# A fused attention and feed-forward kernel: a PSUM bank for the unread products, shared q/k copies, and later zeros

## The chip, the cores and the metric

One core of one Trainium2 chip. The metric is the device time in microseconds (us) of one execution; the median of several executions is compared. Profiles are of one further execution, and their times count from the first instruction of the program.

## What is computed

Chunked attention, and a gated feed-forward layer on its output. There are 4 batches, 8 heads, 768 positions of 64 elements, and 8 memory rows per head. A chunk of 32 queries sees the 8 memory rows and a window of keys from 16 before the chunk to 8 after it.

```
for c in range(nc):
    k_full = concat([mem_k, k[:, :, l_start:r_end]])
    v_full = concat([mem_v, v[:, :, l_start:r_end]])
    a = softmax(scale * q_c @ k_full.T)
    out[:, :, c_start:c_end] = a @ v_full
x = out.transpose(0, 2, 1, 3).reshape(3072, 512)
return (relu(x @ w_gate) * (x @ w_val)) @ w_out
```

The inputs are float32; w_gate and w_val are 512 x 1536, w_out is 1536 x 512. The sizes of chunk and windows are constants of the reference.

## The kernel before

**Tiles.** The 3,072 rows of x are 24 tiles of 128 rows (a = 0 to 23), six a batch. For each tile TensorE transposes q and k into PSUM (`qk_t`, L271; in the first batch two tiles at a time from one load, `pair_t`, L232), ScalarE or VectorE copies them to qT and kT (`qk_copy`, `pair_copy`), TensorE makes the scores (`scores`, L297, 32 small matmuls), VectorE takes the maximum (L322) and subtracts it (L329), ScalarE exponentiates (L337), VectorE sums (L341), inverts (L345) and normalises to p_n (L352). TensorE transposes p_n (L358), a copy makes pT, and TensorE multiplies with the values (`values`, L368) into xT_ps, which is copied to xT. The first batch's values are not loaded into their place by a DMA: they come as natural tiles v_n, are shifted by products with a banded identity (`shift`, L204) and copied into v_q, which lies in v_bd[0]; the memory values come in through vmem_0 (L374). For the later batches the values lie block-diagonal in v_bd[0] and v_bd[1], which must be zero beside the blocks: zeros (`zero`, L130), a load of 32 rows of each window by GpSimd's DMA queue (`load_v_rows`, L182), copies of 24 rows by VectorE (`upper`, L190), and the memory rows (`mem_rows`, L164; in batch 1 from SyncE's queue).

**Feed-forward.** Tiles go in eight blocks of 2 or 4. For a block and each of 12 slices of 128 of the 1,536 columns, TensorE makes g_ps and v_ps (`first`, L401, four matmuls each), ScalarE the relu (L413) and VectorE the product gvT (L419). Then each tile's output is 12 matmuls with w_out (L432), a copy by ScalarE and a store issued by ScalarE (L439).

**PSUM.** Eight banks: pool fps has 4 (g_ps, v_ps, out_ps, vs_ps), sps has 2 that hold one tile of scores, s_all (L138), and aps has 2 (all transposes and xT_ps).

**The order of the work** is made ahead by a planner in the kernel (`schedule`, L683): every piece is an `op` with its engines and planned costs in us, what it depends on, a priority tuple (smaller first), and what it takes from and gives back to `room`, the planned number of free buffers. The planner walks through planned time and gives each engine, whenever it is free, the first ready op. Its result is one fixed order of instructions for each engine; on the chip each engine works through its order and waits by semaphores. GpSimd issues the loads in the order of the list `loads` (L640 to L676), at most 8 in flight.

**Unread products.** While TensorE has nothing ready between planned times 1.3 and WARM = 22 (L678), the planner puts in matmuls of a zero tile `idle` (L468) whose result nobody reads (L141, L751). They write columns 256 to 383 of the second half of s_all; the scores use columns 0 to 255 of both halves.

**Zeros.** v_bd[1] is zeroed at the start in four pieces, one a head pair, by VectorE or ScalarE (`z1`, L470). Of v_bd[0], head pair 2 is zeroed at the start too (`z0`, L471); pairs 3, 0 and 1 hold the memory pattern and v_q until the first batch has used them, and are zeroed later in three pieces each (L472 to L475).

```
op("vm0", {"DVE": 0.5}, lambda e: nc.vector.tensor_copy(vmem_0, vmem_f), [("vml", 1.8)], prio=(-3,))
```

This copies the memory pattern, which SyncE's queue loads (`vml`), to vmem_0; `new_batch` (L259) copies the memory keys into kT before a batch's keys.

Of the kernel before, what the change touches and what calls it, by code (L numbers as in the profile page):

```python
# [19 lines left out]
def kernel(  # L20
# [12 lines left out]
    nc = tc.nc  # L33
# [50 lines left out]
    band = const.tile([128, BAND0 + 176], F16, name="band")  # L84
    ident_h = band[:, BAND0:BAND0 + 128]
    ident_b = const.tile([128, 128], BF16, name="ident_b")
    idle = const.tile([128, 128], BF16, name="idle")
    ident_f = const.tile([128, 128], F32, name="ident_f")
    w_gate_sb = const.tile([128, NFC, DFF], F16, name="w_gate_sb")
    w_val_sb = const.tile([128, NFC, DFF], F16, name="w_val_sb")  # L90
# [44 lines left out]
        else:  # L135
            eng.memset(x.rearrange("p c d -> p (c d)"), 0.0)

    s_all = sps.tile([128, 2, 512], F32, name="s_ps")  # L138

    def idle_product(N):  # L140
        nc.tensor.matmul(s_all[:, 1, 256:256 + N], lhsT=idle, rhs=idle[:, 0:N], start=True, stop=True)  # L141


    def mem_load():
# [151 lines left out]

    def scores(a):  # L297
        b, t = divmod(a, TPB)
        s = s_all
        keys = kT[b].rearrange("p h c s -> p h (c s)")  # L300
        for h2 in range(HP):
            m, par = h2 % 2, h2 // 2
            for g in range(4):
                c = 4 * t + g
                lo, hi = max(KW * c - 16, 0), min(KW * c + 48, NCH * KW)
                o0 = 64 * (2 * m + par) + lo - (KW * c - 16)
                for r in range(2):
                    d = slice(D * r, D * r + D)
                    nc.tensor.matmul(s[CH * g:CH * g + CH, r, o0:o0 + hi - lo],  # L309
                                     lhsT=qT[b][d, h2, CH * c:CH * c + CH],  # L310
                                     rhs=keys[d, h2, lo:hi], start=True, stop=True)
        S_ps[a] = s.rearrange("p a (h s) -> p a h s", s=64)[:, :, 0:HP, :]
# [154 lines left out]

    op("idle", {"DVE": 0.2}, lambda e: nc.vector.memset(idle, 0.0), prio=(-10,))  # L468
    for hp in range(HP):
        op(("z1", hp), {"DVE": 1.5, "ACT": 1.6}, lambda e, hp=hp: zero(engine[e], v_bd[1], hp), ["idle"], prio=(-1, hp), after=["warm2", "vmem_f"] + ["ib"] * (hp > 0))  # L470
    op(("z0", HP - 2), {"DVE": 1.5, "ACT": 1.6}, lambda e: zero(engine[e], v_bd[0], HP - 2), ["idle"], prio=(-1, HP), after=["ib", ("z1", 0)])  # L471
    for hp in (HP - 1, 0, 1):  # L472
        for c0 in range(0, NCH, 8):
            op(("z0", hp, c0), {"ACT": 0.6, "DVE": 0.55}, lambda e, hp=hp, c0=c0: zero(engine[e], v_bd[0], hp, c0, c0 + 8),
               ["vm0" if hp == HP - 1 else ("v", TPB - 1)], prio=(3, -hp) if hp == HP - 1 else (0.7, hp), after=[("v", 3)])  # L475
    op("warm", {"DVE": 0.15}, lambda e: nc.vector.memset(warm, 0.0), prio=(-9,))
    op("warm2", {"ACT": 1.5}, lambda e: nc.scalar.activation(warm, warm, ACT.Exp), ["warm"], prio=(-9,))
    op("vmem_f", {"DVE": 0.55}, lambda e: nc.vector.memset(vmem_f, 0.0), prio=(-8,), after=["warm"])
# [4 lines left out]
    op("kmt", {"PE": 0.25}, lambda e: mem_keys_t(), [("kml", 1.8), "if"], prio=(-5,), take=["aps"])  # L483
    op("kmc", {"ACT": 0.35}, lambda e: nc.scalar.copy(kmemT.rearrange("p b h m -> p (b h m)"), TMP.pop("kmem")),
       ["kmt"], prio=(-5,), give=["aps"])
    op("vm0", {"DVE": 0.5}, lambda e: nc.vector.tensor_copy(vmem_0, vmem_f), [("vml", 1.8)], prio=(-3,))
    for b in range(B):
        op(("new", b), {"DVE": 0.4}, lambda e, b=b: new_batch(b), ["kmc"], take=["kv"],
           prio=(-4.5,) if b == 0 else (1, TPB * b - 2, 0), after=[("t", TPB * b - 2, 0)] if b else [])
# [31 lines left out]
    for a in range(NT):  # L521
        b, t = divmod(a, TPB)
        last = t == TPB - 1
        for i in (1, 0):
            if b == 0:
                if t % 2 == 0:
                    for j in range(2):
                        op(("t", a + j, i), {"PE": 0.3}, lambda e, a=a, i=i, j=j: pair_t(a // 2, i, j),
                           [("pl", a // 2, i), "ib", ("new", b)], (1, a - i, -2 + j), ["aps"])
                        op(("tc", a + j, i), psum16(HP * 128), lambda e, a=a, i=i, j=j: pair_copy(a // 2, i, j, engine[e]),  # L530
                           [("t", a + j, i)], (1, a - i, -2 + j), (), ["aps"])
                continue
            if a >= LATE_QK:
                op(("t", a, i), {"SP": ISSUE}, lambda e, a=a, i=i: qk_transfer(a, i),
                   [(("qk", a, i), SLACK), ("new", b)],
                   (1, a - i, 0), ["kt"] if i else [], [("qk", LAND)], pace_t(a))
                if i:
                    op(("tc", a, i), {"DVE": (0.2, 0.29), "ACT": (0.52, 0.62)}, lambda e, a=a, i=i: qk_copy(a, i, engine[e]),
                       [(("t", a, i), LAND)], (1, a - i, 0), (), ["kt"])
                continue  # L540
            op(("t", a, i), {"PE": 0.24}, lambda e, a=a, i=i: qk_t(a, i), [("qk", a, i), "ib", ("new", b)],
               (1, a - i, 0), ["aps"], ["qk"], pace(max(a - i, 0)))
            op(("tc", a, i), psum16(HP * 128), lambda e, a=a, i=i: qk_copy(a, i, engine[e]), [("t", a, i)],
               (1, a - i, 0), (), ["aps"])
# [116 lines left out]
    for i in range(2):  # L661
        load(("wo", i), 768, 4.1, lambda i=i: load_out(i))
    for b in range(1, B):
        deps = ([("z0", HP - 2)] + [("z0", hp, c0) for hp in (HP - 1, 0, 1) for c0 in range(0, NCH, 8)] if b > 1 else [("z1", hp) for hp in range(HP)]) + ([("v", TPB * (b - NSET + 1) - 1)] if b > NSET else [])
        if b == 1:
            for n in range(2 * HP):
                op(("mr", b, n), {"SP": 0.72}, lambda e, n=n: mem_rows(nc.sync, 1, n),
                   deps + [(("vm", 0), 0.2), (("vm", 1), 0.2)], (0,))
        for par in range(2):
            load_v_op(b, par, deps)  # L670
        if b > 1:
            for n in range(2 * HP):
                load(("mr", b, n), 192, 0.22, lambda b=b, n=n: mem_rows(nc.gpsimd, b, n),
                     deps + [(("vm", 0), 0.2), (("vm", 1), 0.2)])
        for a, i in late[5 if b == 1 else 9 + 12 * (b - 1):21 + 12 * (b - 1)]:
            load_qk_op(a, i)  # L676

    WARM = 22.0  # L678

    def timed(d):  # L680
        return isinstance(d, tuple) and len(d) == 2 and isinstance(d[1], float)
# [1 line left out]
    def schedule():  # L683
        done, started, times = {}, set(), [0.7]
        free = {e: 0.7 for e in ("PE", "ACT", "DVE", "SP", "POOL")}
        queue_end, flying, gives = 0.0, [], []
        todo = {e: [] for e in free}
        order, n_load = [], 0
        names = lambda o: [d[0] if timed(d) else d for d in o["deps"]] + o["after"]
# [23 lines left out]
        while len(started) < len(ops) + len(loads):  # L713
# [8 lines left out]
            while moved:  # L722
                moved = False
                for e in ("POOL", "PE", "ACT", "DVE", "SP"):
                    if free[e] > t + 1e-9:
                        continue
                    if e == "POOL":
                        if n_load == len(loads):
                            continue
                        o = loads[n_load]  # L730
                        if len(flying) >= 8 or not ready(o, t):
                            continue
                        n_load += 1
                        key = o["key"]
                        if o["n"]:
                            end = t + 0.62 + 0.27e-3 * o["n"]
                            queue_end = max(queue_end, end + 0.8) + o["work"]
                            flying.append(queue_end + 1.0)
                            done[key] = queue_end + (1.2 if n_load < 8 else 2.4 if n_load < 45 else 6.0 if key[0] == "vl" else 4.0)
                        else:  # L740
                            end = done[key] = t + max(o["work"], 0.6)
                        fn = o["fn"]
                    else:
                        o = None
                        for _, key in todo[e]:
                            late_pe = e == "PE" and t > 36.0 and ops[key]["prio"][0] == 1
                            if ready(ops[key], t, MARGIN if late_pe else 0.0):
                                o = ops[key]
                                break
                        if o is None:  # L750
                            if e == "PE" and 1.3 < t < WARM:  # L751
                                order.append((t, lambda: idle_product(128)))
                                free[e] = t + (0.107 if t < 9.0 else 0.06)
                                heapq.heappush(times, free[e])
                            elif e == "PE" and t <= 1.3:
                                heapq.heappush(times, 1.31)
                            continue
# [62 lines left out]
```

## Time and profile before

| | |
|---|---|
| device time, three executions | 246.74, 247.69, 246.75 us; median 246.75 |
| the profiled execution | 248.35 us |
| its span, first to last instruction | 246.6 us |
| TensorE clock granted over the span | 1.0 |
| unread products (L141) in the trace | 152, busy 13.4 us |

In a profile, PE is TensorE's matmul, PEld its weight load, DVE VectorE, ACT ScalarE, POOL GpSimd and SP SyncE. A timeline row has the start, the duration, the engine, the line and operation, what is written and read, how many instructions were merged, and in brackets how long the engine had been idle before and what ended that; "issue" means that the profile shows nothing that it waited for. A row of waits has the sum, the number and the longest. The page shows the span in 40 slices of 6.17 us as digits, tenths of busy time. A windows row has the stretch, its length, and for PE, PEld, DVE, ACT and POOL the busy time and the number of instructions. A DMA queue row has packets, MB and the share of 16 engines.

### The profile page before, as it was taken

What the parts mean: (1) busy time and instruction counts of PE and PEld (TensorE: products, weight loads), DVE (VectorE), ACT (ScalarE), POOL (GpSimd) and SP (SyncE); (2) the same over time, 40 slices, a digit from 0 to 9 for tenths busy, and PEclk for the clock granted to TensorE, in tenths of its full rate; (3) what the DMA queues carried; (4) which work ended last, traced back from release to release, by engine and by line L of the source; (5) the groups of instructions that cost most, each with busy time, mean ns of one, the idle gap of its engine ahead of it and who ended that gap; (6) DMA issues with size and microseconds to landing.
All of it is one profiled execution on the core that took longest, in us unless ns stands there. A gap on an engine that the chain in (4) does not pass through costs nothing.

```text
span 246.6 us, 6706 instructions
## 1 busy us (share of the span) xinstructions
PE 237.7 (96%) x2789; PEld 145.2 (59%) x2789; DVE 154.4 (63%) x313; ACT 121.0 (49%) x269; POOL 77.5 (31%) x102
## 2 busy tenths in 40 slices
PE   7969799999999999999999999999999999999994
PEld 6858688887558744555544545554445444444873
DVE  5364687897989739999558999996342034320430
ACT  6564665967446435666325654463332232312432
POOL 8885779212985269319160000000000000000000
PEclk9999999999999999999999999999999999999999
DMA  6999999999999949999996421562001210002102
GB/s 70 173 178 202 201 160 155 191 133 113 147 187 181 102 98 129 131 130 165 103 190 91 45 45 23 130 130 45 3 0 41 90 43 0 0 27 103 43 3 85
DMA packets 96414, 25.19 MB, mean 102 GB/s; under 512 B 87424, under 2 KB 93312, under 8 KB 96384
## 3 DMA queue, kind: packets, MB, share of 16 engines
q0 software_dynamic: 76128, 14.65, 82.1%
q1 hardware_dynamic: 16656, 3.82, 15.1%
q10 hardware_dynamic: 3600, 6.29, 7.9%
q8 instruction: 22, 0.36, 0.6%
q14 instruction: 8, 0.07, 0.1%
HBM read 28.55 MB, written 6.29 MB: 141 GB/s over the span
## 4 chain that ended last, share of the span: by engine, by line
PE 93%; DVE 3%; DMA 1%; issue 1%; ACT 0%; SPq 0%; ACTq 0%
PE v_ps L407 26%; PE g_ps L407 26%; PE out_ps L432 24%; PE s_ps L141 4%; PE xT_ps L388 3%; PE s_ps L309 2%; PE qk_ps L275 2%; PE qk_ps L236 2%; PE pT_ps L358 2%; PE xT_ps L381 1%; PE vs_ps L215 1%; DMA kmem_f<-in_mem_k_dram 1%; PE xT_ps L374 1%; DVE mx L322 1%; DVE dif L329 1%
## 5 line engine op out<-in xcount | busy, mean ns | idle before, releaser
L419 DVE TENSOR_TENSOR gvT<-v_ps,g_relu 128x256 f16<-128x256 f32 (+1 forms) x96 | 52.9, 554 | 54.3 <-PE v_ps L407 40.8
L407 PE MATMUL v_ps<-xT,w_val_sb 128*128 128x256 f16 (+1 forms) x384 | 78.2, 326 | 0.0
L407 PE MATMUL g_ps<-xT,w_gate_sb 128*128 128x256 f16 (+1 forms) x384 | 78.1, 326 | 0.0
L413 ACT ACTIVATE g_relu<-g_ps 128x256 f16<-128x256 f32 (+1 forms) x96 | 47.2, 493 | 52.4 <-PE g_ps L407 51.1
L432 PE MATMUL out_ps<-w_out_sb,gvT 128*128 128x512 f16 (+2 forms) x300 | 65.8, 371 | 0.0
L407 PEld LDWEIGHTS <-w_gate_sb 128*128 128x128 f16 x384 | 36.4, 98 | 23.0
L407 PEld LDWEIGHTS <-w_val_sb 128*128 128x128 f16 x384 | 36.1, 98 | 22.4 <-issue 0.2
L432 PEld LDWEIGHTS <-gvT 128*128 128x128 f16 x300 | 27.8, 98 | 29.4
L79 ACT COPY o_sb<-out_ps 128x512 f32<-128x512 f32 (+2 forms) x25 | 14.2, 568 | 38.4 <-PE out_ps L432 28.3
L337 ACT ACTIVATE p_exp<-dif 128x256 f16<-128x256 f32 (+2 forms) x72 | 19.7, 343 | 10.4 <-DVE dif L329 9.9
L322 DVE TENSOR_REDUCE mx<-s_ps 128x8 f32<-128x512 f32 x24 | 16.5, 687 | 5.3 <-PE s_ps L309 4.8
L254 POOL DMA_DIRECT2D qk_b<-in_q_dram x18 | 16.3, 903 | 11.2 <-DMA v_bd<-in_v_dram 8.5
L81 DVE COPY v_bd<-v_bd 24x768 f16<-24x768 f16 (+1 forms) x48 | 18.0, 415 | 2.7 <-DMA v_bd<-in_v_dram 2.1
L254 POOL DMA_DIRECT2D qk_b<-in_k_dram x18 | 16.3, 908 | 5.2 <-DMA w_out_sb<-in_moe_w_out_dram 3.8
L341 DVE TENSOR_REDUCE sm<-p_exp 128x8 f32<-128x512 f16 x24 | 16.3, 677 | 2.3 <-ACT p_exp L337 2.1
L329 DVE TENSOR_TENSOR dif<-s_ps,mx 128x512 f32<-128x512 f32 x24 | 16.4, 682 | 0.9 <-PE s_ps L141 0.6
L352 DVE TENSOR_TENSOR p_n<-p_exp,rinv 128x512 f16<-128x512 f16 x24 | 16.5, 686 | 0.4
L141 PE MATMUL s_ps<-idle 128*128 128x128 bf16 x152 | 13.4, 254 | 3.0 <-DVE dif L329 1.6
L168 POOL DMA_DIRECT2D v_bd<-vmem x16 | 10.4, 658 | 15.6 <-DMA v_bd<-in_v_dram 15.1
L185 POOL DMA_DIRECT2D v_bd<-in_v_dram x12 | 11.0, 924 | 9.9 <-DVE dif L329 9.2
L141 PEld LDWEIGHTS <-idle 128*128 128x128 bf16 x152 | 11.6, 116 | 4.1 <-issue 2.4
L79 ACT CAST xT<-xT_ps 128x512 f16<-128x512 f32 x16 | 9.3, 583 | 6.9 <-PE xT_ps L388 3.8
(56 smaller groups left out, 172.3 us busy)
## 6 DMA issues: line engine op xcount, KB each, us to landing
out_dram<-o_sb ACTq DMA_DIRECT2D x23, 256.0 KB
qk_b<-in_k_dram POOLq DMA_DIRECT2D x18, 128.0 KB, 7.3
qk_b<-in_q_dram POOLq DMA_DIRECT2D x18, 128.0 KB, 7.0
v_bd<-in_v_dram POOLq DMA_DIRECT2D x6, 384.0 KB, 13.1
w_out_sb<-in_moe_w_out_dram POOLq DMA_DIRECT2D x2, 768.0 KB, 11.0
qk_p<-in_k_dram POOLq DMA_DIRECT2D x3, 256.0 KB, 5.8
qk_p<-in_q_dram POOLq DMA_DIRECT2D x3, 256.0 KB, 6.6
v_n<-in_v_dram POOLq DMA_DIRECT2D x6, 128.0 KB, 7.0
```

What stands on the lines that cost most here:

```text
L79: nc.scalar.copy(o, i)
L81: eng.tensor_copy(o, i)
L141: nc.tensor.matmul(s_all[:, 1, 256:256 + N], lhsT=idle, rhs=idle[:, 0:N], start=True, stop=True)
L254: nc.gpsimd.dma_start(qk_b[a, i], bass.AP(tensor=x.tensor, offset=x[b, 0, 128 * t, 0].offset, ap=[[D, 128], [S * D, H], [1, D]]))
L322: nc.vector.reduce_max(SM[a, "mx"], s4, axis=AX.X)
L329: nc.vector.tensor_tensor(out=SM[a, "dif"].rearrange("p (m r) a s -> p r m a s", r=2), in0=S_ps.pop(a).rearrange("p r (m a) s -> p r m a s ...
L337: nc.scalar.activation(p[:, :, :, s0:s0 + k1 - k0], dif[:, :, :, k0:k1], ACT.Exp, scale=SCALE)
L352: nc.vector.tensor_tensor(out=P_n[a], in0=SM.pop((a, "p")), in1=rinv_b, op=ALU.mult)
L407: nc.tensor.matmul(ps, lhsT=w[:, f, 128 * m:128 * m + 128], rhs=xTs[blk][:, f, :], start=(f == 0), stop=(f == NFC - 1))
L413: nc.scalar.activation(st["r", m], st.pop((0, m)), ACT.Relu)
L419: nc.vector.tensor_tensor(out=st["gv"][:, m, :], in0=st.pop((1, m)), in1=st.pop(("r", m)), op=ALU.mult)
L432: nc.tensor.matmul(st["o", t, c], lhsT=st["gv"][:, m, 128 * t:128 * t + 128], rhs=w_out_sb[:, m, c[0]:c[1]], start=(m == 0), stop=(m == ND ...
```

## The change

The unread products get a buffer of fps of their own, and 256 columns instead of 128; the planner counts one fps buffer less until just after WARM, which is 18 instead of 22. The scores take their tile from the pool for each tile instead of one fixed tile. For the first pair of tiles the copies of the first half go to ScalarE and those of the second half to VectorE. The early zeros of v_bd[1] are assigned to engines by head pair, and the zeros of head pair 2 of v_bd[0] move from the start to the later pieces. The copy to vmem_0 has another priority.

```diff
-    idle = const.tile([128, 128], BF16, name="idle")
+    idle = const.tile([128, 256], BF16, name="idle")
-    s_all = sps.tile([128, 2, 512], F32, name="s_ps")
-
     def idle_product(N):
-        nc.tensor.matmul(s_all[:, 1, 256:256 + N], lhsT=idle, rhs=idle[:, 0:N], start=True, stop=True)
+        if "idle" not in TMP:
+            TMP["idle"] = fps.tile([128, 512], F32, tag="fps", name="idle_ps")
+        nc.tensor.matmul(TMP["idle"][:, 0:N], lhsT=idle[:, 0:128], rhs=idle[:, 0:N], start=True, stop=True)
     def scores(a):
-        s = s_all
+        s = sps.tile([128, 2, 512], F32, name="s_ps")
     for hp in range(HP):
-        op(("z1", hp), {"DVE": 1.5, "ACT": 1.6}, ..., prio=(-1, hp), after=["warm2", "vmem_f"] + ["ib"] * (hp > 0))
-    op(("z0", HP - 2), {"DVE": 1.5, "ACT": 1.6}, lambda e: zero(engine[e], v_bd[0], HP - 2), ["idle"], ...)
-    for hp in (HP - 1, 0, 1):
+        op(("z1", hp), {"ACT": 1.5} if hp % 2 else {"DVE": 1.4}, ..., after=["warm2", "vmem_f"] + ["ib"] * (hp == 2))
+    for hp in (2, 3, 0, 1):
         for c0 in range(0, NCH, 8):
             op(("z0", hp, c0), {"ACT": 0.6, "DVE": 0.55}, ...,
-               ["vm0" if hp == HP - 1 else ("v", TPB - 1)], prio=(3, -hp) if hp == HP - 1 else (0.7, hp), after=[("v", 3)])
+               ["vm0" if hp > 1 else ("v", TPB - 1)], prio=(3, -hp) if hp > 1 else (0.7, hp), after=[("v", 3)])
-    op("vm0", {"DVE": 0.5}, ..., [("vml", 1.8)], prio=(-3,))
+    op("vm0", {"DVE": 0.5}, ..., [("vml", 1.8)], prio=(1, 0, 4.5))
-                        op(("tc", a + j, i), psum16(HP * 128), ...
+                        op(("tc", a + j, i), psum16(HP * 128) if t else {("ACT", "DVE")[j]: psum16(HP * 128)[("ACT", "DVE")[j]]}, ...
-    WARM = 22.0
+    WARM = 18.0
-        queue_end, flying, gives = 0.0, [], []
+        queue_end, flying, gives = 0.0, [], [(WARM + 0.15, "fps")]
+        room["fps"] -= 1
+        heapq.heappush(times, WARM + 0.15)
-                                order.append((t, lambda: idle_product(128)))
-                                free[e] = t + (0.107 if t < 9.0 else 0.06)
+                                order.append((t, lambda: idle_product(256)))
+                                free[e] = t + (0.213 if t < 9.0 else 0.11)
```

The loads of the later batches' values depend on the zeros as before, with the new pieces in the list. "..." within a line stands for text that is the same on both sides. Because the planner runs again, the orders change elsewhere too. The changed program has 69 unread products instead of 152; from the middle of the third batch's attention on, the orders on TensorE are the same.

More of the change, by code (lines that the diff above doesn't have):

```diff
@@ L469 @@
     for hp in range(HP):
-        op(("z1", hp), {"DVE": 1.5, "ACT": 1.6}, lambda e, hp=hp: zero(engine[e], v_bd[1], hp), ["idle"], prio=(-1, hp), after=["warm2", "vmem_f"] + ["ib"] * (hp > 0))
-    op(("z0", HP - 2), {"DVE": 1.5, "ACT": 1.6}, lambda e: zero(engine[e], v_bd[0], HP - 2), ["idle"], prio=(-1, HP), after=["ib", ("z1", 0)])
-    for hp in (HP - 1, 0, 1):
+        op(("z1", hp), {"ACT": 1.5} if hp % 2 else {"DVE": 1.4}, lambda e, hp=hp: zero(engine[e], v_bd[1], hp), ["idle"], prio=(-1, hp), after=["warm2", "vmem_f"] + ["ib"] * (hp == 2))
+    for hp in (2, 3, 0, 1):
         for c0 in range(0, NCH, 8):
             op(("z0", hp, c0), {"ACT": 0.6, "DVE": 0.55}, lambda e, hp=hp, c0=c0: zero(engine[e], v_bd[0], hp, c0, c0 + 8),
-               ["vm0" if hp == HP - 1 else ("v", TPB - 1)], prio=(3, -hp) if hp == HP - 1 else (0.7, hp), after=[("v", 3)])
+               ["vm0" if hp > 1 else ("v", TPB - 1)], prio=(3, -hp) if hp > 1 else (0.7, hp), after=[("v", 3)])
     op("warm", {"DVE": 0.15}, lambda e: nc.vector.memset(warm, 0.0), prio=(-9,))
@@ L485 @@
        ["kmt"], prio=(-5,), give=["aps"])
-    op("vm0", {"DVE": 0.5}, lambda e: nc.vector.tensor_copy(vmem_0, vmem_f), [("vml", 1.8)], prio=(-3,))
+    op("vm0", {"DVE": 0.5}, lambda e: nc.vector.tensor_copy(vmem_0, vmem_f), [("vml", 1.8)], prio=(1, 0, 4.5))
     for b in range(B):
@@ L529 @@
                            [("pl", a // 2, i), "ib", ("new", b)], (1, a - i, -2 + j), ["aps"])
-                        op(("tc", a + j, i), psum16(HP * 128), lambda e, a=a, i=i, j=j: pair_copy(a // 2, i, j, engine[e]),
+                        op(("tc", a + j, i), psum16(HP * 128) if t else {("ACT", "DVE")[j]: psum16(HP * 128)[("ACT", "DVE")[j]]}, lambda e, a=a, i=i, j=j: pair_copy(a // 2, i, j, engine[e]),
                            [("t", a + j, i)], (1, a - i, -2 + j), (), ["aps"])
@@ L663 @@
     for b in range(1, B):
-        deps = ([("z0", HP - 2)] + [("z0", hp, c0) for hp in (HP - 1, 0, 1) for c0 in range(0, NCH, 8)] if b > 1 else [("z1", hp) for hp in range(HP)]) + ([("v", TPB * (b - NSET + 1) - 1)] if b > NSET else [])
+        deps = ([("z0", hp, c0) for hp in range(HP) for c0 in range(0, NCH, 8)] if b > 1 else [("z1", hp) for hp in range(HP)]) + ([("v", TPB * (b - NSET + 1) - 1)] if b > NSET else [])
         if b == 1:
```

## The prediction

> **What bounds the kernel now.** I read the page first, then TensorE's own waits, then the timeline of the stages where it waits.
>
> ```profile
> PE 237.7 (96%) x2789; PEld 145.2 (59%) x2789; DVE 154.4 (63%) x313; ACT 121.0 (49%) x269; POOL 77.5 (31%) x102
> ...
> PE   7969799999999999999999999999999999999994
> ...
> DMA  6999999999999949999996421562001210002102
> ...
> L432 PE MATMUL out_ps<-w_out_sb,gvT 128*128 128x512 f16 (+2 forms) x300 | 65.8, 371 | 0.0
> ...
> L141 PE MATMUL s_ps<-idle 128*128 128x128 bf16 x152 | 13.4, 254 | 3.0 <-DVE dif L329 1.6
> ```
>
> TensorE is busy 96% of a span of 246.6 us. Only the first five slices (31 us) have digits below 9, and part of what they count as busy is the 152 unread products of line 141. After that TensorE waits almost never, so a change can gain only by starting the dense part earlier, and only if nothing later takes it back. The DMA row matters for that: from the second slice to 123 us the engines are 90% busy or more in all slices but one, so loads land when the queue has got to them, not when TensorE is ready. The waits of TensorE over the whole span:
>
> ```profile
> PE s_ps L141 <- DVE dif L329: 1.6, 2, 0.8
> PE s_ps L309 <- issue: 1.5, 1, 1.5
> ...
> PE pT_ps L358 <- DVE p_n L352: 0.5, 1, 0.5
> ```
>
> The unread products stand in the bank that the softmax reads, and wait for its subtraction twice (1.6 us). One stall of 1.5 us has no releaser. One wait of 0.5 us, far later, is for the normalised weights p_n. These three places are the prediction.
>
> **Part 1: the products in their own bank, and the copies.** The start, in order of time:
>
> ```profile
> 7.39 0.29 DVE L263 COPY kT<-kmemT 128x768 bf16<-128x768 bf16 x1
> 7.61 0.65 DVE L486 CAST vmem<-v_bd 128x512 f16<-128x512 f32 x1
> 8.59 1.33 ACT L79 COPY kT<-qk_ps 128x512 bf16<-128x512 bf16 x2 [1.81 <-PE qk_ps L236]
> 10.00 1.35 ACT L79 COPY qT<-qk_ps 128x512 bf16<-128x512 bf16 x2
> 13.47 0.69 DVE L329 TENSOR_TENSOR dif<-s_ps,mx 128x512 f32<-128x512 f32 x1 [0.36 <-PE s_ps L141]
> 13.70 0.77 ACT L79 COPY kT<-qk_ps 128x512 bf16<-128x512 bf16 x1
> 14.21 1.17 PE L141 MATMUL s_ps<-idle 128*128 128x128 bf16 x18 [0.78 <-DVE dif L329]
> 15.31 0.31 PE L309 MATMUL s_ps<-kT,qT 64*32 64x64 bf16 x32
> 17.36 0.69 DVE L329 TENSOR_TENSOR dif<-s_ps,mx 128x512 f32<-128x512 f32 x1 [0.27 <-PE s_ps L141]
> 18.10 1.72 PE L141 MATMUL s_ps<-idle 128*128 128x128 bf16 x28 [0.78 <-DVE dif L329]
> 18.19 0.69 DVE L352 TENSOR_TENSOR p_n<-p_exp,rinv 128x512 f16<-128x512 f16 x1
> 19.66 0.39 PE L358 MATMUL pT_ps<-band,p_n 128*128 128x128 f16 x4
> 20.44 0.74 DVE L81 COPY qT<-qk_ps 128x512 bf16<-128x512 bf16 x1 [0.58 <-PE qk_ps L236]
> 25.63 0.61 PE L407 MATMUL g_ps<-xT,w_gate_sb 128*128 128x256 f16 x4
> ```
>
> The shared copies: two of four move to VectorE, at 0.74 us each (20.44 row), and run beside ScalarE's. The second q copy no longer queues behind the first, but its transposes still need a free bank, so at most some 0.35 us (half of one ScalarE copy) is won at the first scores. Against it, the cast to vmem_0 now stands ahead of the first copy into kT on VectorE, and waits there for the landing of the mem_v pattern; behind it are that copy and TensorE's first transposes. The trace bounds this between nothing and 0.65 us (the whole cast). I take the two as cancelling; ends +0.3 and -0.35.
>
> The bank: the subtraction of 13.47 loses its 0.36, and the second scores (15.31) no longer stand behind 18 products that could not begin before 14.21; they can begin when the key copy of 13.70 ends, at 14.47, so near 14.65: 0.65 us earlier. The second subtraction loses 0.27 more, so p_n of 18.19 ends near 18.0 instead of 18.88. Its transposes, at 19.66 behind 28 products, now stand behind 21 of 256 columns that start near 15.75. A product of 256 columns is not in the trace; it costs between one and two of 128 (1.72/28 = 0.061 us), and I take 0.11, nearest to two: 2.3 us, so the transposes start near 18.15. Between them and the first values stand six more such products and eight transposes; the values gain 1.0, not 1.5. The q copy that VectorE did at 20.44 goes to ScalarE, and the second tile follows its own chain of p_n, aps bank and copy: the first FFN product (25.63) comes **0.8 us earlier** (bounds 0.3 and 1.2). The last products (planned end 18 instead of 22) leave holes, and nothing waits on a product.
>
> **Part 2: the stall without a releaser.**
>
> ```profile
> 0.00:27.33 27.33, 23.51 (x478) 20.14 (x478) 15.06 (x27) 16.88 (x31) 20.39 (x33) 1.00 1.44 160
> 27.33:28.80 1.47, 0.00 (x0) 0.00 (x0) 0.73 (x2) 0.56 (x3) 0.82 (x2) 1.00 1.32 200
> ...
> q8 instruction: 1, 0.02, 16.7%
> ...
> q8 instruction: 22, 0.36, 0.6%
> ```
>
> The first two rows are busy time by window: TensorE stops after 478 matmuls and 478 weight loads, in the middle of a tile's scores. The others are the DMA view of 26.25 to 26.6 us and the page: one of 22 instruction transfers of 16 KB ran just before, and 0.36 MB is 64 bytes for each of TensorE's 5,578 instructions, so 256 a transfer. I read the stall as TensorE out of instructions, its refill late in a busy DMA queue. The changed kernel has 83 products fewer (69 for 152), so 166 instructions fewer by then: the boundary at 956 moves out of dense small matmuls into the third tile's values, past some seven groups of four FFN matmuls. The boundary before it, 256 instructions earlier, falls in the third key transposes, but its refill is asked for while TensorE still runs the slow products. Price: between the old 1.5 at the new place and nothing. I take 0.3 left, so 1.2 won, and TensorE is **2.0 us ahead at 30 us**.
>
> **Part 3: the zeros.**
>
> ```profile
> 36.64 0.61 ACT L134 COPY v_bd<-idle 128x512 f32<-128x512 f32 x1
> ```
>
> One of the five early pieces goes (its engine waited for loads then anyway) and becomes three of 0.61 us, three in a row on ScalarE near 37 us, ahead of a relu. Behind that relu wait a gate product and a bank of fps. TensorE has two FFN groups (0.61 us each, the 25.63 row) and a tile's values to run meanwhile, against 3 x 0.61 = 1.83: even without the values at most 0.6 is lost. With 2.0 in hand I count nothing, for the next part hides it; without that cover it would be these 0.6.
>
> **Part 4: what is late next.** In the stage of 60 to 72 us:
>
> ```profile
> 61.68 1.57 DVE L81 COPY v_bd<-v_bd 24x768 f16<-24x768 f16 x4 [0.99 <-DMA v_bd<-in_v_dram]
> 62.12 0.38 ACTq L439 DMA_DIRECT2D out_dram<-o_sb  x1
> 64.24 0.55 PE L388 MATMUL xT_ps<-pT,v_bd 128*128 128x32 f16 x16
> 69.19 0.69 DVE L352 TENSOR_TENSOR p_n<-p_exp,rinv 128x512 f16<-128x512 f16 x1
> 69.94 0.40 PE L358 MATMUL pT_ps<-band,p_n 128*128 128x128 f16 x4 [0.46 <-DVE p_n L352]
> 71.02 0.69 DVE L329 TENSOR_TENSOR dif<-s_ps,mx 128x512 f32<-128x512 f32 x1
> ```
>
> VectorE waits 0.99 us for the values of the second batch, which land near 61.65, and then works without a gap until p_n ends at 69.88: 8.2 us of row copies and softmax. GpSimd issued these loads near 40 us, behind loads that do not depend on TensorE, and DMA is full; so the landing stays. Both orders have the same 16 row copies, maximum, subtraction, sum, reciprocal and product there. TensorE coming 2.0 us early waits at the values of 64.24 (until about 63.4) and again at 69.94. The gain is lost but for what the new order puts ahead of 69.94: three more out_ps matmuls, 3 x 65.8/300 = 0.65 us.
>
> That 0.65 is then spent. Behind the transposes of 69.94 the new order has the next scores ahead of the next tile's weight transposes, and these scores need a key copy on ScalarE. From the end of the subtraction (71.71) ScalarE has to do:
>
> ```profile
> 71.75 0.81 ACT L337 ACTIVATE p_exp<-dif 128x256 f16<-128x256 f32 x3 [0.78 <-DVE dif L329]
> 72.47 0.56 ACT L79 COPY o_sb<-out_ps 128x512 f32<-128x512 f32 x1
> 73.06 0.34 ACTq L439 DMA_DIRECT2D out_dram<-o_sb  x1
> 73.45 0.38 ACT L413 ACTIVATE g_relu<-g_ps 128x256 f16<-128x256 f32 x1 [0.42 <-PE v_ps L407]
> 74.47 0.60 ACT L79 COPY kT<-qk_ps 128x512 bf16<-128x512 bf16 x1
> ...
> 75.46 0.39 PE L358 MATMUL pT_ps<-band,p_n 128*128 128x128 f16 x4
> ```
>
> Exponents 0.81, relu 0.38, output copy 0.56, its store 0.34, an xT copy (0.56, as the output copy) and the key copy 0.60: 3.25 us, to 75.0. Scores of 0.31 follow, then the transposes at about 75.6; they stood at 75.46 with about as much done (no scores ahead, but one FFN group more). So the whole change is worth between -0.65 and +0.3 us there. With the copies overlapping at their ends, as they do in these rows, I take **-0.15**. Afterwards TensorE had no wait to shorten, and the orders agree again.
>
> The profiled execution took 248.35 us, 1.75 beyond its span and 1.6 above the median of 246.75; the sum moves it to 248.2, and the median to **246.6**.
>
> **The rivals.** (a) *The gain passes through.* If the values land earlier than I read, or VectorE's 8.2 us shrink, the 2.0 us of part 2 reach the end: 246.35 for the profiled execution, 244.7 for the median. For it: the wait is only 0.99 us. Against: the full DMA row.
>
> (b) *Slower: the output store meets the values' load.* The store of 62.12 comes just after the landing of 61.65. With TensorE ahead by more than 0.5 us it is issued before it and shares the engines with the load that everything waits for.
>
> ```profile
> q10 hardware_dynamic: 3600, 6.29, 7.9%
> ```
>
> The 24 tiles' stores keep 16 engines for 7.9% of the span, 19.5 us, so one for 0.8 us. Two stores before the landing cost up to 1.6 us of VectorE's chain: with -0.15, up to 1.45 later, 248.2. It decides once the lead exceeds 0.5 us. The Trainium skill (DMA: Bandwidth & Descriptors, Queues, rings and completion order) says that each DMA engine takes turns between the queues that it has work for, a packet at a time. By that rule the store would not wait behind the load but delay it, as in (b); no run here shows a store beside this load.
>
> (c) *The change doesn't do what it says*: the stall stays whole, or products wait in fps. Then TensorE is some 0.5 us ahead at 30 us, and part 4 gives the same end: 246.4 to 246.8.
>
> **How the numbers follow.** The median can be told from no change by about 0.5%, 1.2 us. My sum, its bounds (246.1 to 247.05) and (c) lie within that: 0.65. (a) is faster by 0.8%: 0.19. (b) needs both stores, or one and a full ScalarE queue, for more than 1.2 us: 0.16. The range leaves out the full size of (a) and reaches most of (b): 245.2 to 248.0.
>
> **What would show it.** Right: no product waits for dif or mx; first FFN near 24.8; TensorE's stall of 1.5 gone; VectorE's wait for v_bd grown from 0.99 to about 3 us; transposes still near 69.9. Wrong: a v_bd landing clearly before 61; row copies much shorter than 0.4 us each; a new stall of TensorE without a releaser; or TensorE short of banks behind the zeros near 38 us.

## The result, and the profile after

The changed kernel takes 245.95 us (median of 10 executions, 244.85 to 246.7), the kernel before 247.07 us in the same comparison (10 executions, 246.32 to 247.8). The ratio is 0.9949, with a 95% interval of 0.993 to 0.9969: 1.1 us faster. The interval lies wholly below 1, so the gain is clear of the noise, though single executions of one kernel differ by more than it (1.5 to 1.9 us). It lies at the 0.5% which the prediction drew as its border for "no change". The medians here and below are of all executions; each ratio leaves disturbed ones out and sets a kernel against executions of before that were taken beside it (medians 246.79 to 247.13 us), so medians and ratios need not agree to the last tenth.

The page of the changed kernel, with the lines that answer to those of before:

```profile
PE 235.3 (96%) x2706; PEld 140.5 (57%) x2706; DVE 154.0 (63%) x313; ACT 122.0 (50%) x271; POOL 77.7 (32%) x102
...
PE   7898999999889999899999999999999999999994
...
DMA  6999999999999999999993121443001210002102
...
q8 instruction: 21, 0.34, 0.7%
...
L432 PE MATMUL out_ps<-w_out_sb,gvT 128*128 128x512 f16 (+2 forms) x300 | 66.0, 371 | 0.0
...
L141 PE MATMUL idle_ps<-idle 128*128 128x256 bf16 x69 | 10.7, 302 | 1.1 <-DVE warm L475 1.1
```

The span is 244.9 us, the profiled execution 246.7 us, the slowest of the ten. The idle 3.0 us ahead of the unread products have become 1.1, at the program's start. New digits of 8 stand in the 11th, 12th and 17th slice (61 to 73 and 98 to 104 us): what was won early is partly waited away there. TensorE's waits say where:

```profile
PE pT_ps L358 <- DVE p_n L352: 1.0, 1, 1.0
PE qk_ps L236 <- issue: 0.8, 1, 0.8
PE qk_ps L275 <- ACT xT L79: 0.8, 1, 0.8
...
PE xT_ps L388 <- DVE v_bd L81: 0.4, 1, 0.4
```

No product waits for dif. A stall without a releaser is still there, shorter, at other instructions. Three waits are new or longer. The timeline rows:

```profile
12.98 0.31 PE L309 MATMUL s_ps<-kT,qT 64*32 64x64 bf16 x32
14.00 2.47 PE L141 MATMUL idle_ps<-idle 128*128 128x256 bf16 x21
16.30 0.39 PE L358 MATMUL pT_ps<-band,p_n 128*128 128x128 f16 x4
22.74 0.47 PE L236 MATMUL qk_ps<-ident_b,qk_p 128*64 128x128 bf16 x9 [0.84 <-issue]
23.14 0.61 PE L407 MATMUL g_ps<-xT,w_gate_sb 128*128 128x256 f16 x4
59.40 1.57 DVE L81 COPY v_bd<-v_bd 24x768 f16<-24x768 f16 x4 [1.55 <-DMA v_bd<-in_v_dram]
66.92 0.69 DVE L352 TENSOR_TENSOR p_n<-p_exp,rinv 128x512 f16<-128x512 f16 x1
67.67 0.40 PE L358 MATMUL pT_ps<-band,p_n 128*128 128x128 f16 x4 [1.04 <-DVE p_n L352]
102.62 0.38 PE L275 MATMUL qk_ps<-ident_b,qk_b 128*128 128x128 bf16 x4 [0.78 <-ACT xT L79]
```

The first FFN product starts at 23.14 instead of 25.63. The values of batch 1 landed at 59.38, not 61.66, and p_t(7), the transposes of the eighth tile's p_n, stand where VectorE's chain behind that landing ends: 67.67 - 59.38 = 8.29 us, as it was 69.94 - 61.66 = 8.28 before.

### The profile page after: what moved, and what is told of

It is laid out like the page before. It is cut to its first block, busy times and chain, and to the rows that moved or that the text cites. A ratio compares the mean times of both kernels' runs of the same rounds, so it can differ in the third digit from the quotient of the medians.

```text
span 244.9 us, 6549 instructions
## 1 busy us (share of the span) xinstructions
PE 235.3 (96%) x2706; PEld 140.5 (57%) x2706; DVE 154.0 (63%) x313; ACT 122.0 (50%) x271; POOL 77.7 (32%) x102
## 4 chain that ended last, share of the span: by engine, by line
PE 63%; DMA 18%; DVE 8%; POOL 5%; issue 3%; ACT 2%; ACTq 0%; POOLq 0%; DVEq 0%
PE out_ps L432 21%; PE g_ps L407 19%; PE v_ps L407 18%; DMA v_bd<-in_v_dram 8%; DMA qk_p<-in_q_dram 6%; DMA w_gate_sb<-in_moe_w_gate_dram 4%; DVE v_bd L81 3%; PE xT_ps L388 2%; PE s_ps L309 1%; DVE gvT L419 1%; POOL v_n L199 1%; DVE dif L329 1%; POOL qk_p L227 1%; DVE mx L322 1%; PE pT_ps L358 1%
## 5 line engine op out<-in xcount | busy, mean ns | idle before, releaser
L388 PEld LDWEIGHTS <-v_bd 128*128 128x128 f16 x288 | 9.8, 96 | 4.0 <-DVE v_bd L81 0.7
L141 PE MATMUL idle_ps<-idle 128*128 128x256 bf16 x69 | 10.7, 302 | 1.1 <-DVE warm L475 1.1
```

## The experiments

Theory at the start: the products made the early gain; the landing of batch 1's values, with VectorE's 8.3 us behind it, takes part of it back. Rivals: the copies or the zeros made the gain; the difference of the landings is all there is.

**The kernel before, a second time** (no edit).

> The kernel before once more, unchanged, for a second trace. Theory (the 61.66 at which batch 1's values landed in the first trace was one late execution): it lands between 58 and 60.7, the time is 246 to 247.5 in place of 248.35, the transposes p_t(7) stand at 68.0 to 69.6 without a long wait, and the stall of about 1.5 us at the 956th instruction is there again. Rival (the old order of work makes the values late): the landing is at 61.2 or later again, and the time is near 248.

```profile
24.68 0.61 PE L407 MATMUL g_ps<-xT,w_gate_sb 128*128 128x256 f16 x4
27.73 0.23 PE L309 MATMUL s_ps<-kT,qT 64*32 64x64 bf16 x9 [1.36 <-issue]
57.90 2.98 DVE L81 COPY v_bd<-v_bd 24x768 f16<-24x768 f16 x9
61.46 0.69 DVE L322 TENSOR_REDUCE mx<-s_ps 128x8 f32<-128x512 f32 x1 [0.58 <-PE s_ps L309]
68.56 0.40 PE L358 MATMUL pT_ps<-band,p_n 128*128 128x128 f16 x4 [0.15 <-DVE p_n L352]
```

247.19 us. The values landed at 59.15, VectorE made nine row copies without waiting for them, and then waited for TensorE's scores. The rows that the prediction read were thus those of a late execution, in its start (first FFN product 25.63 against 24.68) and in its landing. In the twelve traces whose load order was not edited the landing lies between 57.58 and 61.66, and 61.66 is the latest. From here on the changed kernel is set against this trace. It is one trace too: two traces of the same kernel differ by 0.95 us at the first FFN product, so less than that between two single traces says little.

**Parts of the change, one alone or one undone.** The products alone:

```diff
 # before, with the new idle, idle_product, scores and room, WARM = 18.0, and
-                                order.append((t, lambda: idle_product(128)))
+                                order.append((t, lambda: idle_product(256)))
```

> Before, with the unread products alone changed (a bank of their own, 256 columns, planned end 18); copies, cast and zeros as before. Theory: the early gain comes from the products, so the first FFN product of tile 0 starts within 0.6 us of the changed kernel's 23.1 (before 25.6), and the refill stall stands in the third key transposes near 22.7 instead of in the scores at 28.8. The time is then within 0.4 us of the changed kernel's 245.95. Rival (the shared copies made the gain): first FFN product above 24.8, time 246.7 to 247.1. Rival (the landing of batch 1's values decides and varies from run to run): it lands anywhere from 59 to 62, and the transposes p_t(7) stand 8.2 us behind it whatever the early gain.

The change with the products as before:

```diff
+    s_all = sps.tile([128, 2, 512], F32, name="s_ps")
...
-                                order.append((t, lambda: idle_product(256)))
+                                order.append((t, lambda: idle_product(128)))
-    WARM = 18.0
+    WARM = 22.0
```

> The changed kernel with its unread products put back: 128 columns, in the bank of the scores, planned end 22. Theory: first FFN product back to 25.0 or later, products wait for dif again, the stall without a releaser (about 1.5 us) is back near the fourth scores, and the time is back within 0.4 us of 247.07. Rival (the copies): first FFN product stays below 24, time below 246.2. Rival (the landing): the time follows the landing, not the start.

The change with the copies as before:

```diff
-    ... psum16(HP * 128) if t else {("ACT", "DVE")[j]: ...}, ...
+    ... psum16(HP * 128), ...
-    op("vm0", ..., prio=(1, 0, 4.5))
+    op("vm0", ..., prio=(-3,))
```

> The changed kernel with the first tiles' copies left to the planner and the cast to vmem_0 early again. Theory: they cancel, so first FFN product within 0.4 us of 23.1 and time within 0.4 us of 245.95. Rival (the copies made the gain): first FFN product 24.5 or later, time above 246.5.

The change with the zeros as before, and the zeros alone:

```diff
+    op(("z0", HP - 2), {"DVE": 1.5, "ACT": 1.6}, lambda e: zero(engine[e], v_bd[0], HP - 2), ...)
-    for hp in (2, 3, 0, 1):
+    for hp in (HP - 1, 0, 1):
...
```

> The changed kernel with the zeros as before (one early zero of the second head pair, copies of it gone from 37 us). Theory: nothing, time within 0.4 us of 245.95. Rival (the three zeros on ScalarE near 37 us cost a relu): 0.4 to 0.6 us faster. Rival (an early zero in front of the first copies costs the start): first FFN product 0.5 us or more later than 23.1, time above 246.4.

> The kernel before with the zeros alone changed; products, copies and cast as before. The run with the zeros undone came out no faster than before, so they may be worth something. Theory (they are worth nothing, the difference was the spread of the runs): within 0.4 us of before's 246.9. Rival (the zeros carry a good part of the gain): 0.6 to 1.0 us faster, with the first scores or the stage from 37 to 56 us shorter by as much.

| kernel | median us | ratio to before (95%) | first FFN product | 11th gate product | landing | p_t(7) |
|---|---|---|---|---|---|---|
| before, second trace | 247.19 (one) | | 24.68 | 38.43 | 59.15 | 68.56 |
| changed | 245.95 | 0.9949 (0.993 to 0.9969) | 23.14 | 35.38 | 59.38 | 67.67 |
| products alone | 245.97 | 0.9965 (0.9938 to 0.9993) | 23.28 | 35.47 | 57.94 | 66.29 |
| products undone | 246.81 | 0.999 (0.9962 to 1.0018) | 23.89 | 37.78 | 59.07 | 68.07 |
| copies undone | 245.96 | 0.9958 (0.9929 to 0.9987) | 23.54 | 35.72 | 59.31 | 67.60 |
| zeros undone | 246.51 | 0.9997 (0.9976 to 1.0017) | 23.07 | 35.26 | 57.58 | 66.74 |
| zeros alone | 247.63 | 1.0017 (0.9989 to 1.0045) | 24.59 | 38.17 | 58.26 | 68.59 |

The landing is that of the second half of batch 1's values, for which VectorE's row copies wait. The products alone give the lead (35.47 against 38.43 at the eleventh gate product) and a gain, and undoing them takes the gain away, as the theory had it, though the intervals of the two overlap; only the first FFN product came back to 23.89, not to 25.0. The waits with the products undone:

```profile
PE s_ps L141 <- DVE dif L329: 1.6, 2, 0.8
PE vs_ps L215 <- issue: 1.4, 1, 1.4
```

Both are back. The copies make no difference that can be told. For the zeros the runs disagree: alone they bring nothing (1.0017), but undoing them took the gain away (0.9997), against the expectation. The products alone have the old zeros too and keep their gain, so the zeros aren't needed for it; the intervals of these two runs overlap. The trace of the zeros undone is as early as the changed kernel's at the eleventh gate product, and earlier at p_t(7), but its execution (245.9 us) was one of the faster of twelve. No row shows why, and it stays open.

**Count against bank.** The bank of its own, but 128 columns and WARM as before, 142 products (with WARM the planner also holds the fps buffer back until 22.15 instead of 18.15):

```diff
-                                order.append((t, lambda: idle_product(256)))
-                                free[e] = t + (0.213 if t < 9.0 else 0.11)
+                                order.append((t, lambda: idle_product(128)))
+                                free[e] = t + (0.107 if t < 9.0 else 0.06)
-    WARM = 18.0
+    WARM = 22.0
```

> The changed kernel with 142 products of 128 columns (planned end 22) in place of 69 of 256, still in a bank of their own. Theory (the refill of 256 instructions at a time sets TensorE's pace in this stage): no product waits for dif, but 146 instructions more bring the stall of about 1.5 us back to the 956th instruction, 27 to 29 us, and none stands in the third key transposes; time 0.3 to 0.8 us above the changed kernel's 245.95. Rival (the waits for dif and mx were all of the gain): no stall, time within 0.3 us of the changed kernel.

Its timeline, then its busy time by window (the last three numbers are the granted clock, the DMA share and GB/s):

```profile
21.54 0.52 PE L381 MATMUL xT_ps<-pT,v_bd 56*64 56x32 f16 x22 [0.68 <-issue]
...
27.74 1.28 PE L215 MATMUL vs_ps<-v_n,band 128*64 128x256 f16 x11 [2.33 <-issue]
28.95 1.03 PE L407 MATMUL v_ps<-xT,w_val_sb 128*128 128x256 f16 x4
```

```profile
27.74:31.45 3.71, 3.71 (x23) 2.55 (x24) 1.36 (x3) 1.55 (x3) 3.13 (x4) 0.54 1.32 200
```

247.27 us, ratio 0.9979 (0.9945 to 1.0012). Nothing waits for dif, and the first FFN product is at 23.46, 1.2 us ahead of the second trace of before. Then TensorE stands 2.33 us and goes on at 27.74, where before went on at 27.73: in this trace the refill of instructions took back all that the bank had won at the start. The rival (no stall) is out. Behind the stall the granted clock is 0.54 for 3.71 us, and four FFN matmuls take 1.03 us instead of 0.61.

The times say less than the trace. The median is 1.3 us above the changed kernel's, where 0.3 to 0.8 was expected, but the twelve executions fall into two halves. In six, the traced one (248.84) among them, the mean granted clock is 0.991 to 0.993, and they take 247.37 to 250.42 us. In the other six it is 0.999 or 1.0, and they take 245.42 to 247.18, the middle 245.6: no slower than the changed kernel. So 142 products cost time in the executions in which the clock fell; that they cost any in the others isn't shown, and none of those was traced.

**Fewer instructions still.** 36 products of 512 columns, the 256 zeros read twice:

```diff
-    nc.tensor.matmul(TMP["idle"][:, 0:N], lhsT=idle[:, 0:128], rhs=idle[:, 0:N], ...)
+    nc.tensor.matmul(TMP["idle"][:, 0:N], lhsT=idle[:, 0:128],
+                     rhs=bass.AP(tensor=idle.tensor, offset=idle.offset,
+                                 ap=[idle.ap[0], [0, N // 256], [1, 256]]), ...)
-                                order.append((t, lambda: idle_product(256)))
-                                free[e] = t + (0.213 if t < 9.0 else 0.11)
+                                order.append((t, lambda: idle_product(512)))
+                                free[e] = t + (0.426 if t < 9.0 else 0.22)
```

> The changed kernel with 36 products of 512 columns (the 256 zeros read twice) in place of 69 of 256. Theory of the refill: 66 instructions fewer, so the 702nd instruction lies in the fourth scores, some 2 us later in TensorE's work, its refill is there in time (it was asked for at 20.4 and could be used at 22.7), and the stall of 0.84 us in the third key transposes goes; first FFN product 0.5 to 0.9 us ahead of 23.1. At the end 0 to 0.9 us faster, by how much the later gate takes back. Rival (that stall is not the refill's): it stays at the same transposes. Rival (longer products stand in the way): first FFN product 0.3 us later or more.

```profile
21.87 0.61 PE L408 MATMUL g_ps<-xT,w_gate_sb 128*128 128x256 f16 x4
...
23.84 0.28 PE L310 MATMUL s_ps<-kT,qT 64*32 64x64 bf16 x21 [0.32 <-issue]
...
66.38 0.40 PE L359 MATMUL pT_ps<-band,p_n 128*128 128x128 f16 x4 [0.58 <-DVE p_n L353]
```

245.12 us (six executions), ratio 0.991 (0.9883 to 0.9937). The stall has moved to the fourth scores, as the count of instructions says, and shrunk to 0.32; it did not go altogether, because this refill also began later. The lead is 1.27 us more than the changed kernel's, and p_t(7) still waits 0.58 for p_n.

When the 16 KB refill packets (q8, instruction, in the DMA view) began, and when TensorE went on, in ten traces:

| kernel | products | refill began | TensorE went on | idle by the row |
|---|---|---|---|---|
| before | 152 | 26.30 | 28.80 | 1.47 |
| before, second trace | 152 | 25.23 | 27.73 | 1.36 |
| products undone | 142 | 24.71 | 27.20 | 1.4 |
| zeros alone | 145 | 25.15 | 27.50 | 1.2 |
| bank, 128 columns | 142 | 25.24 | 27.74 | 2.33 |
| changed | 69 | 20.39 | 22.74 | 0.84 |
| products alone | 73 | 20.48 | 22.77 | 0.83 |
| copies undone | 70 | 20.72 | 23.13 | 0.5 |
| zeros undone | 72 | 20.27 | 22.61 | 0.5 |
| 512 columns | 36 | 21.51 | 23.84 | 0.32 |

In every row TensorE goes on 2.3 to 2.5 us after the refill's packets begin, whatever the kernel, the bank or the length of the stall; the four traces that are not in the table agree. The first five stand at the 956th instruction, the others at the 700th to 702nd: some 256 apart. That TensorE runs out of instructions, which the prediction only read from one trace, is by these runs as good as shown.

That the full DMA makes the refill late is not tested by an edit, but the first trace of before fits it. Its third refill ends the stall at 956, so each further one stands for 256 instructions more. The third began 55 instructions before TensorE needed it. The 20th, at 192.16 us, where the DMA is nearly idle (share 0.08 from 186 to 221 us), began some 320 before.

The stall also comes back further on in kernels that are early: without a releaser, and 256 instructions apart, TensorE waits 0.52 us at 45.11 and 0.28 at 52.95 with 512 columns, 0.20 at 44.76 and 0.55 at 52.33 with the zeros undone, and 0.71 at 52.27 with the products alone, each 2.3 to 2.8 us after a refill began. So the refill can be a limit well behind the start.

**The landing as the gate.** Two further loads ahead of the values, in the changed kernel and in the kernel before; all other orders stay:

```diff
+    order = schedule()
+    vals = [(n, 1, par) for par in range(2) for n in ("vl", "ve")]
+    seq1 = vals + late[5:5 + 2]
+    seq2 = late[5:5 + 2] + vals
...
```

> The changed kernel with batch 1's four value loads issued behind two further q/k loads on GpSimd's queue, all other orders the same. Theory (the landing is a gate once TensorE is early): second half lands 1.4 to 2.0 us later than otherwise, p_t(7) stands 8.2 us behind the landing, and the time is 0.7 to 2.0 us above 245.95. Rival (the landing is hidden behind TensorE's own work): less than 0.4 us slower. Rival (the landing comes where the queue pleases from run to run): no relation, and the landing anywhere from 57.5 to 62.

> The kernel before with batch 1's value loads issued behind two further q/k loads, as in values_late. Theory (before, TensorE is some 2 us later and covers part of a late landing): 0 to 0.7 us above before's 246.9, less than the 1.2 us that the same edit cost the changed kernel. Rival (the landing is the gate of both kernels alike): 1.0 us or more above before. Rival (the landing is never the gate): within 0.2 us in both, which the run of values_late already speaks against.

The timeline of the changed kernel with late values, and a row of its windows:

```profile
62.45 0.80 PE L388 MATMUL xT_ps<-pT,v_bd 128*128 128x32 f16 x12 [2.25 <-DVE v_bd L81]
...
66.10 3.17 PE L432 MATMUL out_ps<-w_out_sb,gvT 128*128 128x512 f16 x9
```

```profile
64.60:69.20 4.60, 4.60 (x20) 1.91 (x17) 4.32 (x10) 1.94 (x5) 4.60 (x6) 0.63 2.18 158
```

Changed: 247.12 us, ratio 1.0002 (0.9973 to 1.0031) against 0.9949 without the edit, so 1.3 us dearer: the landing is a gate there. Its trace shows more than the theory. The landing is at 62.02, 2.6 us later than in the changed kernel's trace (1.4 to 2.0 was expected). Some 2 us behind a wait of 2.25 us the granted clock is 0.63 for 4.60 us, nine out_ps matmuls take 3.17 us instead of some 2.1, and TensorE, not p_n, is late at p_t(7) (70.75; p_n ends at 69.57). But this execution (249.34 us) is one of four with a mean clock of 0.993; the other eight, at 0.999 or 1.0, took 246.45 to 247.66 us, the middle 0.8 above the changed kernel. So the late landing costs time without the clock too, and more with it. Before: 248.32 us, ratio 1.0059 (1.0032 to 1.0085), 1.4 us dearer. I expected 0 to 0.7, because before's slack in the second trace is 68.56 - 59.15 - 8.3 = 1.1 us of the 1.4 to 2.0 by which I took the landing to move. The expectation missed, and what came is the rival (the gate of both kernels alike, 1.0 us or more); its one trace (landing at 60.64 only, a late start) does not show where the 1.4 us go. So the landing matters for both kernels, and the size for before is not explained.

**VectorE's chain behind the landing.** Four of the sixteen row copies on ScalarE, in the changed kernel and in the one with 512 columns:

```diff
-    op(("up", b, n, m), {"DVE": 0.1 + 64 * 0.5e-3 * (i1 - i0)},
+    op(("up", b, n, m), {"ACT": 0.2 + 64 * 0.79e-3 * (i1 - i0)} if (b, m, n % 2) == (1, 1, 1)
+       else {"DVE": 0.1 + 64 * 0.5e-3 * (i1 - i0)},
```

> The changed kernel with four of the sixteen row copies of batch 1's values (those of the second half of the tiles, odd rows of the list) on ScalarE in place of VectorE. Theory (VectorE's chain from the values' landing to p_n, 8.2 us, is a gate): the chain shrinks by 1.0 to 1.6 us, the transposes p_t(7) no longer wait or wait 0.3 us at most, and the time falls by 0.3 to 1.0 us below 245.95. Rival (TensorE itself is the bound there): chain shorter, same time within 0.3 us. Rival (ScalarE then delays exponents or key copies): slower by 0.3 us or more.

```profile
60.58 1.57 DVE L81 COPY v_bd<-v_bd 24x768 f16<-24x768 f16 x4 [3.01 <-DMA v_bd<-in_v_dram]
65.30 0.38 PE L275 MATMUL qk_ps<-ident_b,qk_b 128*128 128x128 bf16 x4 [1.30 <-DVE qT L81]
66.29 0.69 DVE L352 TENSOR_TENSOR p_n<-p_exp,rinv 128x512 f16<-128x512 f16 x1
67.80 0.40 PE L358 MATMUL pT_ps<-band,p_n 128*128 128x128 f16 x4
```

245.73 us, ratio 0.9937 (0.9912 to 0.9963), not to be told from the changed kernel; the 0.3 to 1.0 us that were expected did not come. The chain is shorter (67.80 - 60.56 = 7.24 us) and p_t(7) does not wait, but TensorE waits 1.30 for a q copy in the same stage: one wait for another, at least in this trace, whose execution (247.14 us) was the slowest of twelve and whose landing is late.

> The changed kernel with 36 products of 512 columns and four of the sixteen row copies on ScalarE, both edits together. Theory (two limits one behind the other, the start by the refill and the chain behind the landing): the gains add in part, time 244.3 to 245.1, p_t(7) within 7.4 us of the landing. Rival (only the start matters): as with 512 columns alone, 245.1 plus or minus 0.2. Rival (the copies on ScalarE hold up key copies, as the 1.3 us wait for qT in that trace): 245.4 or more.

```profile
62.56 0.38 PE L276 MATMUL qk_ps<-ident_b,qk_b 128*128 128x128 bf16 x4 [1.06 <-DVE xT L81]
65.78 0.40 PE L359 MATMUL pT_ps<-band,p_n 128*128 128x128 f16 x4
```

244.36 us, ratio 0.9905 (0.9878 to 0.9933): the best of all, some 2.5 us below before in its comparison, and inside the 244.3 to 245.1 expected. p_t(7) stands 65.78 - 58.06 = 7.72 us behind the landing, not within 7.4: TensorE waits 1.06 us for an xT copy ahead of it. Whether it beats the 512 columns alone (0.991) the ratios do not tell.

## Why the prediction was right, and where it was not

The time came out 0.65 us below the forecast of 246.6 and inside the range, between the forecast and rival (a): an early gain, most of which does not reach the end. That mechanism was right. The size was not: the sum had -0.15 us for the change and 1.1 was measured, and the range of 2.8 us was wide enough to hold both, so that the time fell inside it is partly luck. The steps:

- **Part 1, the bank: right in kind, too small.** First FFN product predicted 0.8 us earlier (0.3 to 1.2). Against the second trace of before it is 1.5, outside the bounds and with the stall already paid; against the first it is 2.5, of which 0.95 is that execution's late start. The term that was mis-sized is the second scores, put 0.65 earlier; with the products alone they come 1.2 earlier (13.14 against 14.36), 0.25 of it already at the first scores (10.09 against 10.34), the rest the 0.78 us wait and products that no longer stand ahead. A product of 256 columns costs 2.47/21 = 0.118 us, predicted 0.11.
- **Part 1, copies and cast: not contradicted.** First FFN product 23.54 with them undone and 23.14 with them, less than two traces of one kernel differ; no effect on the time that the runs can tell.
- **Part 2, the stall: the cause right, the place half right.** The boundary did move into the third key transposes' reach, and that is where the stall went: 0.84 us instead of the 0.3 taken. The refill was not early enough "while TensorE still runs the slow products": it began at 20.39 and could be used at 22.74. The 2.0 us of lead at 30 us were 3.05 at the eleventh gate product (38.43 to 35.38). What the prediction had too small is what the number of products is worth, in the stalls that it moves: 36 products come out 0.8 us faster than 69 (their intervals just overlap), and with the bank but 142 products the traced lead is gone at 27.74 us, though the six executions without the lower clock end as early as the changed kernel.
- **Part 3, the zeros: not settled** (alone nothing, as predicted; undone, against it). The place was right: the three zeros run on ScalarE from 33.61 for 1.65 us, and TensorE does not wait between 33 and 45 us in the changed kernel's trace.
- **Part 4, "so the landing stays": this step failed.** The 61.66 was one late execution, and the sign that was named for it (a landing clearly before 61) came. The chain of 8.2 us and the gate were right: 8.29 us, with the wait of 1.55 us for the values and 1.04 us for p_n. Against the second trace p_t(7) comes 0.89 earlier. That this is close to the 0.65 for the three out_ps matmuls is chance: there before's p_t(7) was 1.1 us later than its values' landing asked for, and the changed kernel took up that slack.
- **Part 4, "that 0.65 is then spent": wrong in place.** Nothing is spent behind p_t(7): p_t(8) comes 1.21 earlier (74.08 to 72.87). ScalarE's work there was sized about right, 3.08 us from the end of the subtraction (69.51) to the end of the key copy (72.59) for the 3.25 summed, and the transposes followed 0.28 us later, where the prediction had 0.6. Part is spent at 102.62, where TensorE waits 0.78 us for ScalarE's xT copy. At the end of these two traces 0.5 us is left (spans 245.4 and 244.9), though the traced execution of the changed kernel was its slowest; the medians differ by 1.1.
- **Rival (b): not borne out, but not tested either.** One store was issued before the values landed at 59.38 (at 57.83), the next at 60.76, behind it. The stores' queue from 56.4 to 62 us:

```profile
q10 hardware_dynamic: 48, 0.09, 6.1%
```

All of these 48 packets come behind the landing: the same view of 56.4 to 60.25 us has none of this queue, and the first begins at 60.30. So the first store's packets came 2.5 us after its issue and never ran beside the load, and no price can be read. The Trainium skill's rule (DMA: Bandwidth & Descriptors, Queues, rings and completion order) that each DMA engine takes turns between the queues that it has work for is not tested by this trace.

## What to carry to other kernels

While DMA is full, count TensorE's instructions, not only their time: fillers half as wide are twice as many, each a matmul and a weight load to fetch, and a gain ahead of a late refill can be waited away at it. Look at the granted clock of every execution before reading a median: here half of one kernel's twelve had a lower one, and half had not. Take a second trace before resting a sum on when one load lands: this one moved by four microseconds between executions and kernels with the same load order. A gain at the start reaches the end only as far as the next gate lets it, so look for that gate in the same change; that shortening the chain behind it pays was not shown here (245.73 against 245.95 us).

## What was not expected of the hardware

- Refills of 256 TensorE instructions began 6.4 us apart while the DMA was full (13.51, 19.94, 26.30 in the first trace of before), and TensorE went on 2.3 to 2.5 us after a refill's packets began. The Trainium skill (Runtime: NRT & Kernel Launch, Instruction fetch mechanics) gives the same 16 KiB blocks of 256 instructions and calls the cost of crossing a boundary mostly hidden; here it was 0.3 to 2.3 us at one boundary, in the ten traces of the table.
- A wait of 2.25 or 2.33 us was followed by a granted clock of 0.63 over 4.6 us and 0.54 over 3.7 us; the wait of 1.04 us at p_t(7) of the changed kernel was followed by matmuls of the usual length. The Trainium skill (TensorE: Matmul & The Clock Gate, Part 1) has the half rate after an idle window of about 3.4 us that runs free of the kernel; the waits here were shorter.
- The same 27 unread products took 3.09 us in the first trace of before (114 ns each, to 7.98 us) and 2.45 us in the second (to 7.04); in the second the products were 107 ns apart until about 6.2 us and 55 ns from there on. Later in the first trace 28 of them took 1.72 us (61 ns each). The granted clock in the profile is 1.00 from 5 to 8 us all the same.
